# Single-query attention over 256 heads: folding K further on VectorE, and routing the last 16 rows of V past the group sum

## The chip, the cores and the metric

The kernel runs on one core of one Trainium2 chip. The time is that of the device, in microseconds (us), from launch to end of the program on that core; the median over several executions is compared. The times before and after are taken on the same chip. Traces are of one profiled execution.

## What is computed

Attention with one query per head: 8 x 32 = 256 heads, 4096 keys and values of 128 elements, all bfloat16. Each head has its own K and V, so every element is read once (268 MB each) and used in two operations.

```python
def reference(q, k, v):
    scale = q.shape[-1] ** -0.5
    scores = jnp.einsum('bhqd,bhkd->bhqk', q, k) * scale
    attn = _softmax(scores, axis=-1)
    return jnp.einsum('bhqk,bhkd->bhqd', attn, v)
```

## The kernel before

**Tiles.** Eight heads make a tile: the 128 partitions are 8 heads x 16 blocks of keys, and each partition holds C = 256 rows of D = 128 elements, so that one tile of K or V is 8.4 MB. There are NT = 32 tiles t of each kind. Three buffers (`kv_pool`, `SLOTS = 3`) hold K and V tiles in turn: the load order is k0, k1, v0, k2, v1, k3, v2 and so on, and each load reuses the buffer of the load three places before it. So V of tile t goes into the buffer of K of tile t, and K of t+1 into that of V of t-2.

**Scores of a tile.** `product` (L187) multiplies a part of K by the query (L191, VectorE, in place) and folds the products along D: it adds the upper half of the 128 to the lower half (L194), and in the second half of the rows once more (L199), so that 64 or 32 partial products are left per row. `width_of` (L182) says how many. The first and the last three tiles always stop at 64. `sum_over_d` (L206) then adds the remaining partial products on TensorE: it multiplies by the identity and accumulates slices of DS = 8 elements of 64 rows into one PSUM bank (128 x 512, L211), so 8 or 4 matmuls for a quarter of the rows. `scores_of` (L220) reduces the 8 sums that are left per row on VectorE (L223). `weights_of` (L232) takes the maximum (L235 to L242), the exponential on ScalarE (L248) and spreads the weights over eight columns, one per head (L255).

**Values.** `values_loop` (L271, tiles 0 to 28) and `values_of` (L307, the last three) multiply four rows of V at a time by the weights: each matmul has 32 stationary columns and 512 moving ones. In `values_loop` all 64 matmuls are accumulated in one group of 32 columns. In `values_of` successive matmuls go to four column groups, j = 0 to 3, which can run beside one another; in the last tile, the 12 matmuls on rows 128 to 175 all go to group 0 (L315). `copy_of` (L347, ScalarE) brings the sums to SBUF, and `result_of` (L354) adds the groups and picks each head's own part with four small matmuls (L367). `finish_of` (L372) divides by the sum of exponentials on ScalarE, `store_of` (L381) writes to memory from ScalarE's queue.

**The last tile.** V of tile 31 arrives in seven pieces of 128, 64, 32, 16, 8, 4 and 4 rows (`cuts`, L146). Its last LAST = 8 rows don't go through the group sum: GpSimd copies their weights into `w_last` (L261), and eight small matmuls of one row each (L361) add them to the result ahead of the picks (L367).

**Order.** The order within TensorE, VectorE, ScalarE and SP is that of the program text (`manual_schedule`, L392). All loads are issued on SP (L158). In the loop stage (t = 1 to 29) VectorE does `product` on the first half, then on the third quarter, then the reductions of the first two quarters, then `product` on the last quarter and its reductions; TensorE does the sums as they become ready and after the last of them the values loop of the tile before; SP issues K of t+1 when that loop's predecessor has freed its buffer, and V of t when the last sum of K of t is done.

Of the kernel before, what the change touches and what calls it, by code (L numbers as in the profile page):

```python
# [8 lines left out]
ALU = mybir.AluOpType  # L9
AX = mybir.AxisListType  # L10
BF16 = mybir.dt.bfloat16
F32 = mybir.dt.float32
# [3 lines left out]
TG = 4  # L16
R = 2
OB = 4
LAST = 8
LOOP = 6  # L20
EDGE = 2
NEG = -1.0e30
# [3 lines left out]
def kernel(  # L26
# [7 lines left out]
    nc = tc.nc  # L34
    B, H, Sq, D = q.shape
    S = k.shape[2]
    P = nc.NUM_PARTITIONS
# [3 lines left out]
    C = S // PH  # L41
    NT = NH // G
    scale = float(D) ** -0.5
    UC = 64
    DS = 512 // UC
    NU = C // UC
    CB = 4
    RG = R * G
    NQ = NT // R
# [1 line left out]
    AG = CB * G  # L51
    NV = C // CB
    assert (NV - 2 * EDGE) % LOOP == 0
    assert LAST % CB == 0 and TG * AG == P and NH % P == 0 and P % G == 0 and TB % PH == 0 and C % CB == 0

# [12 lines left out]
    ps_s = ctx.enter_context(tc.tile_pool(name="ps_s", bufs=3, space=bass.MemoryType.PSUM))  # L68
# [7 lines left out]
    ident = consts.tile([P, P], BF16, name="ident")  # L76
    nc.gpsimd.memset(ident[:], 0.0)
    nc.gpsimd.affine_select(
        out=ident[:], in_=ident[:], pattern=[[-1, P]], compare_op=ALU.not_equal,
# [6 lines left out]
        out=heads[:], in_=heads[:], pattern=[[-1, G], [0, PH]], compare_op=ALU.not_equal,  # L86
# [6 lines left out]
        out=own[:], in_=own[:], pattern=[[-PH, G]], compare_op=ALU.is_ge,  # L93
# [3 lines left out]
        out=own[:], in_=own[:], pattern=[[PH, G]], compare_op=ALU.is_ge,  # L97
# [14 lines left out]
    for j in range(TG):  # L112
        part = pick[j * AG : (j + 1) * AG, :, :, :]
        nc.gpsimd.affine_select(
            out=part, in_=part, pattern=[[-1, CB], [CB * G, R], [-CB, RG]],
# [6 lines left out]
        out=mine[:], in_=mine[:], pattern=[[PH * G, R], [-PH, RG]], compare_op=ALU.is_ge,  # L122
# [3 lines left out]
        out=mine[:], in_=mine[:], pattern=[[-PH * G, R], [PH, RG]], compare_op=ALU.is_ge,  # L126
        fill=0.0, base=PH - 1, channel_multiplier=-1,
    )

    w_last = consts.tile([P, LAST, RG], BF16, name="w_last")  # L130
    nc.gpsimd.memset(w_last[:], 0.0)
# [4 lines left out]
    def behind_loop(made):  # L136

        if loops:
            tc.add_manual_dep(
                made.ins, loops[-1].name,  # L140
                mybir.DependencyInfo(
                    mybir.DependencyClass.NoSync, mybir.DependencyReason.SCHED_ONLY
                ),
            )
# [2 lines left out]
        ("k", 0): [C // 4, C // 4, C // 2],  # L147
        ("k", NT - 2): [C // 2] * 2,
        ("k", NT - 1): [C // 4, C // 4, C // 2],
        ("v", NT - 1): [C // 2, C // 4, C // 8, C // 16, C // 32, LAST // 2, LAST // 2],  # L150
    }

    def load(kind, t):
# [25 lines left out]
        nc.scalar.activation(out=qb[:, 0, :], in_=qp[:], func=ACT.Copy)  # L179
        qbs[t] = qb  # L180

    def width_of(t, u):  # L182


        return D // 4 if u >= NU // 2 and 0 < t < NT - 3 else D // 2

    def product(t, lo, hi):  # L187
        kt = loads["k", t]
        qb = qbs[t]
        part = kt[:, lo:hi, :]  # L190
        nc.vector.tensor_tensor(  # L191
            out=part, in0=part, in1=qb[:].to_broadcast([P, hi - lo, D]), op=ALU.mult
        )
        nc.vector.tensor_tensor(  # L194
            out=part[:, :, 0 : D // 2], in0=part[:, :, 0 : D // 2],
            in1=part[:, :, D // 2 : D], op=ALU.add,
        )
        if width_of(t, lo // UC) < D // 2:
            nc.vector.tensor_tensor(  # L199
                out=part[:, :, 0 : D // 4], in0=part[:, :, 0 : D // 4],  # L200
                in1=part[:, :, D // 4 : D // 2], op=ALU.add,
            )

    sums = {}

    def sum_over_d(t, u):  # L206
        kt = loads["k", t]
        ps = ps_s.tile([P, UC, DS], F32, name="ps", tag="ps")
        n = width_of(t, u) // DS
        for s in range(n):  # L210
            nc.tensor.matmul(  # L211
                ps[:], lhsT=ident[:],
                rhs=kt[:, u * UC : (u + 1) * UC, s * DS : (s + 1) * DS],
                start=(s == 0), stop=(s == n - 1),
            )
        sums[t, u] = ps

    scs = {}

    def scores_of(t, u):  # L220
        if u == 0:
            scs[t] = sc_pool.tile([P, C], F32, name="sc", tag="sc")
        made = nc.vector.tensor_reduce(  # L223
            out=scs[t][:, u * UC : (u + 1) * UC], in_=sums.pop((t, u))[:], axis=AX.X, op=ALU.add
        )
        if u == NU - 1:
            behind_loop(made)

    ws = {}
# [2 lines left out]
    def weights_of(t):  # L232
# [26 lines left out]
        if t == NT - 1:  # L259
            for i in range(LAST // CB):  # L260
                nc.gpsimd.tensor_copy(  # L261
                    out=w_last[:, i * CB : (i + 1) * CB, RG - G : RG].rearrange("p m g -> p g m"),
                    in_=w[:, (C - LAST) // CB + i, :, :],
                )
# [40 lines left out]
    LT = NT - 3  # L305

    def values_of(t, lo, hi):  # L307
        vt = loads["v", t]
        w = ws[t]
        if lo == 0:  # L310
            avs[t] = ps_v.tile([P, CB * D], F32, name="av", tag="av")
        end = C if t < NT - 1 else C - LAST


        group = [  # L315
            0 if t == NT - 1 and C // 2 <= c0 < C // 2 + 3 * C // 16 else c0 // CB % TG
            for c0 in range(0, end, CB)
        ]
        for c0 in range(lo, hi, CB):
            i = c0 // CB  # L320
            j = group[i]
            nc.tensor.matmul(  # L322
                avs[t][j * AG : (j + 1) * AG, :], lhsT=w[:, i, :, :],
                rhs=vt[:, c0 : c0 + CB, :], start=(i < TG), stop=(j not in group[i + 1 :]),
            )
# [28 lines left out]
    def result_of(t):  # L354
        n, r = divmod(t, R)
        comb = combs.pop(t)
        if r == 0:
            ops[n] = ps_o.tile([RG, D], F32, name="op", tag="op")
        if t == NT - 1:
            for i in range(LAST):  # L360
                nc.tensor.matmul(  # L361
                    ops[n][:], lhsT=w_last[:, i, :], rhs=loads["v", t][:, C - LAST + i, :],
                    start=False, stop=False,
                )
        e = AG if t < LT else P
        for m in range(CB):
            nc.tensor.matmul(  # L367
                ops[n][:], lhsT=pick[0:e, m, r, :], rhs=comb[0:e, m, :],
                start=(r == 0 and m == 0), stop=(r == R - 1 and m == CB - 1),
            )  # L370

    def finish_of(n):  # L372
        s, u = divmod(n, OB)
# [11 lines left out]
            lo = u if (last and u == OB - 1) else 0  # L385
            nc.scalar.dma_start(o_n[s, :, lo : u + 1, :], stages[s][:, lo : u + 1, :])

    Q = C // 4

    load("k", 0)  # L390
    E = mybir.EngineType
    with tc.manual_schedule(engines={E.PE, E.DVE, E.Activation, E.SP}):  # L392
        q_prep(0)
        q_prep(1)
        for t in range(NT):
            loop = 0 < t <= LT
            v_last = t >= NT - 2
            n = t // R - 1
            if not loop:
                if t + 1 < NT:  # L400
                    load("k", t + 1)
                load("v", t)
            product(t, 0, 2 * Q if loop else Q)
            if not loop:
                sum_over_d(t, 0)
            if 0 < t - 1 <= LT:
                if (t - 1) % R == 0:
                    norm_of(n)
                if t > 1:
                    result_of(t - 2)  # L410
            if t + 2 < NT:
                q_prep(t + 2)
            if loop:
                sum_over_d(t, 0)
            else:
                product(t, Q, 2 * Q)
            sum_over_d(t, 1)
            if not loop:
                scores_of(t, 0)
            product(t, 2 * Q, 3 * Q)  # L420
            sum_over_d(t, 2)
            if loop:
                scores_of(t, 0)
            scores_of(t, 1)
            if t > 2 and t % R == 1:
                recip_of(n)
            product(t, 3 * Q, C)
            sum_over_d(t, 3)
            scores_of(t, 2)
            if loop:  # L430
                values_loop(t - 1)
                load("k", t + 1)
                load("v", t)
            if v_last:
                values_of(t - 1, 0, C)
            scores_of(t, 3)
            weights_of(t)
            if t > 2 and t % R == 1:
                finish_of(n)
            if t > 0:  # L440
                copy_of(t - 1)
                if t > 2 and t % R == 1:
                    store_of(n)
                if not loop:
                    if t % R == 0:
                        norm_of(n)
                    result_of(t - 1)
        values_of(NT - 1, 0, C // 2)
        norm_of(NQ - 1)
        recip_of(NQ - 1)  # L450
        values_of(NT - 1, C // 2, C - LAST)
        copy_of(NT - 1)
        result_of(NT - 1)
        finish_of(NQ - 1)
        store_of(NQ - 1)
# [30 lines left out]
```

## Time and profile before

| | us |
|---|---|
| median of 14 runs | 1251.71 (1251.57 to 1252.02) |
| the profiled execution's own time | 1252.92 |
| its span, first to last instruction | 1251.2 |
| VectorE busy | 1021.9 |
| TensorE busy (matmuls; loads of weights 301.1) | 792.6 |
| ScalarE busy | 166.0 |
| bytes read | 536.94 MB, mean 429 GB/s over the span |

The busy times of the engines overlap each other, so they don't add up to the span. A busy share over the whole run says which engine could be the limit; whether it is shows in what it waits for in one period of the loop (some 38.7 us) and in the stretch behind the last load. A DMA load of K or V is shared by 16 DMA engines, each of which adds one to the load's semaphore when its share has landed; the load counts as landed at the sixteenth.

### The profile page before, as it was taken

How to read it: one execution, taken by the hardware profiler on the slowest of the kernel's cores; microseconds unless marked ns; L12 is line 12 of the kernel's file. 1: busy time of each engine (PE TensorE's matmuls, PEld its weight loads, DVE VectorE, ACT ScalarE, POOL GpSimd, SP SyncE). 2: the span in 40 equal slices, each digit the busy share in tenths (PEclk: the TensorE clock that was granted, in tenths of full speed). 3: DMA queues.
4: the chain of work that ended last, by engine and by line, in shares of the span. 5: the costliest groups of instructions: out<-in, count | busy, mean ns of one | idle time of the engine just before them, and what ended most of it. 6: DMA issues, size and time to landing. Idle time of an engine off the chain costs nothing. (4 is left out here: it accounts for less than half of the span.)

```text
span 1251.2 us, 10828 instructions
## 1 busy us (share of the span) xinstructions
PE 792.6 (63%) x3110; PEld 301.1 (24%) x3110; DVE 1021.9 (82%) x495; ACT 166.0 (13%) x433; POOL 4.0 (0%) x22
## 2 busy tenths in 40 slices
PE   2466567655576655766557765577655776656756
PEld 0122122222232222322222222222222222222212
DVE  7887987878977789777798777987779877798783
ACT  0111011111011110111101111011110111101111
POOL 1000000000000000000000000000000000000000
PEclk8687788777887778877788777887877878779866
DMA  9999999999999999999999999999999999999997
GB/s 404 436 436 434 436 434 434 434 436 434 436 422 427 434 436 436 428 434 432 436 436 434 432 436 434 430 430 436 434 434 434 428 433 436 434 434 422 427 438 318
DMA packets 11432, 537.33 MB, mean 429 GB/s; under 512 B 1808, under 2 KB 2064, under 8 KB 2320
## 3 DMA queue, kind: packets, MB, share of 16 engines
q1 hardware_dynamic: 11072, 536.94, 99.4%
q8 instruction: 15, 0.25, 0.1%
q10 hardware_dynamic: 336, 0.07, 0.0%
q14 instruction: 9, 0.07, 0.0%
HBM read 536.94 MB, written 0.07 MB: 429 GB/s over the span
## 5 line engine op out<-in xcount | busy, mean ns | idle before, releaser
L191 DVE TENSOR_TENSOR kt<-kt,qb 128x8192 bf16<-128x8192 bf16 (+1 forms) x99 | 560.9, 5665 | 146.6 <-DMA kt<-in_k_dram 139.9
L211 PE MATMUL ps<-kt,ident 128*128 128x512 bf16 x800 | 282.2, 517 | 385.7 <-DVE kt L199 296.8
L294 PE MATMUL av<-vt,w 128*32 x1740 | 425.2, 396 | 4.6
L194 DVE TENSOR_TENSOR kt<-kt 128x4096 bf16<-128x4096 bf16 (+1 forms) x99 | 288.8, 2917 | 3.4
L294 PEld LDWEIGHTS av<-vt,w 128*32 x1740 | 173.0, 99 | 262.5 <-issue 120.3
L211 PEld LDWEIGHTS <-ident 128*128 128x128 bf16 x800 | 96.8, 121 | 564.4 <-issue 529.4
L223 DVE TENSOR_REDUCE sc<-ps 128x64 f32<-128x512 f32 x128 | 85.3, 685 | 53.5 <-PE ps L211 53.5
L248 ACT ACTIVATE e<-sc,nmax 128x256 bf16<-128x256 f32 x32 | 16.2, 508 | 706.4 <-DVE nmax L242 706.4
L255 ACT ACTIVATE w<-e,mine 128x256 bf16<-128x256 bf16 x256 | 105.6, 495 | 1.1
L199 DVE TENSOR_TENSOR kt<-kt 128x2048 bf16<-128x2048 bf16 x56 | 68.6, 1225 | 1.9
L351 ACT ACTIVATE comb<-av 32x512 bf16<-32x512 f32 (+1 forms) x32 | 18.7, 585 | 330.9 <-PEq L284 321.1
L280 PE MATMUL av<-vt,w 128*32 128x512 bf16 x116 | 47.1, 498 | 14.6 <-issue 13.2
L367 PE MATMUL op<-comb,pick 32*16 32x128 bf16 (+1 forms) x128 | 12.1, 213 | 22.1 <-ACT comb L351 22.1
L280 PEld LDWEIGHTS av<-vt,w 128*32 128x32 bf16 x116 | 6.9, 100 | 54.8 <-issue 54.8
L177 PE MATMUL qp<-qg,heads 8*128 8x128 bf16 x32 | 6.9, 216 | 16.8 <-ACT qg L175 16.8
L322 PE MATMUL av<-vt,w 128*32 128x512 bf16 x190 | 16.4, 423 | 0.8 <-DMA vt<-in_v_dram 0.8
L367 PEld LDWEIGHTS <-pick 32*16 32x16 bf16 (+1 forms) x128 | 8.7, 83 | 29.2 <-issue 28.7
L235 DVE TENSOR_REDUCE pmax<-sc 128x1 f32<-128x256 f32 x32 | 13.4, 420 | 1.1
L175 ACT ACTIVATE qg<-qh 8x128 bf16<-8x128 f32 x32 | 8.5, 266 | 33.5 <-PE qh L171 33.5
L171 PE MATMUL qh<-q_all,ident 128*8 128x128 bf16 x32 | 7.2, 224 | 8.6 <-DMA q_all<-in_q_dram 8.3
L179 ACT ACTIVATE qb<-qp 128x128 bf16<-128x128 f32 x32 | 8.9, 277 | 9.7 <-PE qp L177 9.7
L322 PEld LDWEIGHTS <-w 128*32 128x32 bf16 x190 | 6.9, 103 | 9.8 <-issue 5.9
(31 smaller groups left out, 48.1 us busy)
## 6 DMA issues: line engine op xcount, KB each, us to landing
kt<-in_k_dram SPq DMA_DIRECT2D x4, 4096.0 KB, 24.3
kt<-in_k_dram SPq DMA_DIRECT2D x4, 2048.0 KB, 13.3
vt<-in_v_dram SPq DMA_DIRECT2D x1, 4096.0 KB, 35.0
vt<-in_v_dram SPq DMA_DIRECT2D x1, 2048.0 KB, 39.5
vt<-in_v_dram SPq DMA_DIRECT2D x1, 1024.0 KB, 41.5
vt<-in_v_dram SPq DMA_DIRECT2D x1, 512.0 KB, 42.3
vt<-in_v_dram SPq DMA_DIRECT2D x31, 25.8
kt<-in_k_dram SPq DMA_DIRECT2D x29, 28.3
```

The source lines that it names most:

```text
L191: nc.vector.tensor_tensor(out=part, in0=part, in1=qb[:].to_broadcast([P, hi - lo, D]), op=ALU.mult)
L194: nc.vector.tensor_tensor(out=part[:, :, 0 : D // 2], in0=part[:, :, 0 : D // 2], in1=part[:, :, D // 2 : D], op=ALU.add,)
L199: nc.vector.tensor_tensor(out=part[:, :, 0 : D // 4], in0=part[:, :, 0 : D // 4], in1=part[:, :, D // 4 : D // 2], op=ALU.add,)
L211: nc.tensor.matmul(ps[:], lhsT=ident[:], rhs=kt[:, u * UC : (u + 1) * UC, s * DS : (s + 1) * DS], start=(s == 0), stop=(s == n - 1),)
L223: made = nc.vector.tensor_reduce(out=scs[t][:, u * UC : (u + 1) * UC], in_=sums.pop((t, u))[:], axis=AX.X, op=ALU.add)
L248: nc.scalar.activation(out=e[:], in_=sc[:], func=ACT.Exp, bias=nmax[:, 0:1], scale=scale, accum_out=esums[t // R][:, t % R : t % R + 1],)
L255: nc.scalar.activation(out=w[:, :, g, :], in_=e_g, func=ACT.Copy, scale=mine[:, 0, g : g + 1])
L280: pe.matmul(av, lhsT=wf[:, i * nw : (i + 1) * nw], rhs=vf[:, i * nv : (i + 1) * nv], **how)
L294: pe.matmul(av, lhsT=wf[:, bass.ds(ow + i * nw, nw)], rhs=vf[:, bass.ds(ov + i * nv, nv)], start=False, stop=False,)
L322: nc.tensor.matmul(avs[t][j * AG : (j + 1) * AG, :], lhsT=w[:, i, :, :], rhs=vt[:, c0 : c0 + CB, :], start=(i < TG), stop=(j not in group[ ...
L351: nc.scalar.activation(out=comb[0:n, :, :], in_=av[0:n, :, :], func=ACT.Copy)
L367: nc.tensor.matmul(ops[n][:], lhsT=pick[0:e, m, r, :], rhs=comb[0:e, m, :], start=(r == 0 and m == 0), stop=(r == R - 1 and m == CB - 1),)
```

## The change

It has two parts.

*Folding K.* In tiles 1 to 28 the first half and the last quarter of the rows are folded down to 16 partial products per row, where they were folded to 64 and to 32; the third quarter stays at 32. The sums on TensorE take whole parts: the first half (128 rows) goes into one PSUM bank in slices of BANK / 128 = 4 elements, the quarters in slices of 8 as before. In tiles 1 to 28 the first half then takes 4 matmuls (16 before, for its two quarters), the third quarter 4 (as before), the last 2 (4 before). The scores of the first half are reduced by one instruction where there were two, in tile 29 too.

*The last tile.* LAST is 16: the last 16 rows, in pieces of 8, 4 and 4 rows, go straight into the result. The pieces of the load keep their sizes. The matmuls of the last four rows stand behind the four picks, the other twelve ahead of them. Rows 128 to 151 (6 matmuls) go to column group 0, where it was rows 128 to 175 (12 matmuls); 28 matmuls of the second half go through the group sum, where there were 30.

The diff, without the lines that only rename arguments:

```diff
-LAST = 8
+LAST = 16
...
-    UC = 64
-    DS = 512 // UC
-    NU = C // UC
+    BANK = 512
...
-        ("v", NT - 1): [C // 2, C // 4, C // 8, C // 16, C // 32, LAST // 2, LAST // 2],
+        ("v", NT - 1): [C // 2, C // 4, C // 8, C // 16, LAST // 2, LAST // 4, LAST // 4],
...
-    def width_of(t, u):
-        return D // 4 if u >= NU // 2 and 0 < t < NT - 3 else D // 2
+    def width_of(t, lo):
+        return (D // 4 if lo == C // 2 else D // 8) if 0 < t < NT - 3 else D // 2
...
     def product(t, lo, hi):
...
-        nc.vector.tensor_tensor(
-            out=part[:, :, 0 : D // 2], in0=part[:, :, 0 : D // 2],
-            in1=part[:, :, D // 2 : D], op=ALU.add,
-        )
-        if width_of(t, lo // UC) < D // 2:
+        n = D
+        while n > width_of(t, lo):
+            n //= 2
             nc.vector.tensor_tensor(
-                out=part[:, :, 0 : D // 4], in0=part[:, :, 0 : D // 4],
-                in1=part[:, :, D // 4 : D // 2], op=ALU.add,
+                out=part[:, :, 0:n], in0=part[:, :, 0:n], in1=part[:, :, n : 2 * n], op=ALU.add
             )
...
-    def sum_over_d(t, u):
+    def sum_over_d(t, lo, hi):
         kt = loads["k", t]
-        ps = ps_s.tile([P, UC, DS], F32, name="ps", tag="ps")
-        n = width_of(t, u) // DS
+        ps = ps_s.tile([P, BANK], F32, name="ps", tag="ps")
+        ds = BANK // (hi - lo)
+        n = width_of(t, lo) // ds
         for s in range(n):
             nc.tensor.matmul(
-                ps[:], lhsT=ident[:],
-                rhs=kt[:, u * UC : (u + 1) * UC, s * DS : (s + 1) * DS],
+                ps[:], lhsT=ident[:], rhs=kt[:, lo:hi, s * ds : (s + 1) * ds],
                 start=(s == 0), stop=(s == n - 1),
             )
...
-    def scores_of(t, u):
+    def scores_of(t, lo, hi):
...
+        ps = sums.pop((t, lo))[:].rearrange("p (c s) -> p c s", c=hi - lo)
         made = nc.vector.tensor_reduce(
-            out=scs[t][:, u * UC : (u + 1) * UC], in_=sums.pop((t, u))[:], axis=AX.X, op=ALU.add
+            out=scs[t][:, lo:hi], in_=ps, axis=AX.X, op=ALU.add
         )
...
-            0 if t == NT - 1 and C // 2 <= c0 < C // 2 + 3 * C // 16 else c0 // CB % TG
+            0 if t == NT - 1 and C // 2 <= c0 < C // 2 + 3 * C // 32 else c0 // CB % TG
...
-        if t == NT - 1:
-            for i in range(LAST):
+        def last_rows(lo, hi):
+            for i in range(lo, hi):
                 nc.tensor.matmul(
                     ops[n][:], lhsT=w_last[:, i, :], rhs=loads["v", t][:, C - LAST + i, :],
-                    start=False, stop=False,
+                    start=False, stop=(i == LAST - 1),
                 )
-        e = AG if t < LT else P
+
+        if t == NT - 1:
+            last_rows(0, 3 * LAST // 4)
         for m in range(CB):
             nc.tensor.matmul(
                 ops[n][:], lhsT=pick[0:e, m, r, :], rhs=comb[0:e, m, :],
-                start=(r == 0 and m == 0), stop=(r == R - 1 and m == CB - 1),
-            )
+                start=(r == 0 and m == 0), stop=(r == R - 1 and m == CB - 1 and t < NT - 1),
+            )
+        if t == NT - 1:
+            last_rows(3 * LAST // 4, LAST)
...
-            product(t, 0, 2 * Q if loop else Q)
-            if not loop:
-                sum_over_d(t, 0)
+            if loop:
+                product(t, 0, HALF)
+            else:
+                product(t, 0, Q)
+                sum_over_d(t, 0, Q)
...
-                sum_over_d(t, 0)
+                sum_over_d(t, 0, HALF)
...
-            sum_over_d(t, 1)
...
             if loop:
-                scores_of(t, 0)
-            scores_of(t, 1)
+                scores_of(t, 0, HALF)
+            else:
+                scores_of(t, Q, HALF)
```

More of the change, by code (lines that the diff above doesn't have):

```diff
@@ L193, in product @@
         )
-        nc.vector.tensor_tensor(
-            out=part[:, :, 0 : D // 2], in0=part[:, :, 0 : D // 2],
-            in1=part[:, :, D // 2 : D], op=ALU.add,
-        )
-        if width_of(t, lo // UC) < D // 2:
+        n = D
+        while n > width_of(t, lo):
+            n //= 2
             nc.vector.tensor_tensor(
-                out=part[:, :, 0 : D // 4], in0=part[:, :, 0 : D // 4],
-                in1=part[:, :, D // 4 : D // 2], op=ALU.add,
+                out=part[:, :, 0:n], in0=part[:, :, 0:n], in1=part[:, :, n : 2 * n], op=ALU.add
             )
     sums = {}
-    def sum_over_d(t, u):
+    def sum_over_d(t, lo, hi):
         kt = loads["k", t]
-        ps = ps_s.tile([P, UC, DS], F32, name="ps", tag="ps")
-        n = width_of(t, u) // DS
+        ps = ps_s.tile([P, BANK], F32, name="ps", tag="ps")
+        ds = BANK // (hi - lo)
+        n = width_of(t, lo) // ds
         for s in range(n):
             nc.tensor.matmul(
-                ps[:], lhsT=ident[:],
-                rhs=kt[:, u * UC : (u + 1) * UC, s * DS : (s + 1) * DS],
+                ps[:], lhsT=ident[:], rhs=kt[:, lo:hi, s * ds : (s + 1) * ds],
                 start=(s == 0), stop=(s == n - 1),
             )
-        sums[t, u] = ps
+        sums[t, lo] = ps
     scs = {}
-    def scores_of(t, u):
-        if u == 0:
+    def scores_of(t, lo, hi):
+        if lo == 0:
             scs[t] = sc_pool.tile([P, C], F32, name="sc", tag="sc")
+        ps = sums.pop((t, lo))[:].rearrange("p (c s) -> p c s", c=hi - lo)
         made = nc.vector.tensor_reduce(
-            out=scs[t][:, u * UC : (u + 1) * UC], in_=sums.pop((t, u))[:], axis=AX.X, op=ALU.add
+            out=scs[t][:, lo:hi], in_=ps, axis=AX.X, op=ALU.add
         )
-        if u == NU - 1:
+        if hi == C:
             behind_loop(made)
@@ L358, in result_of @@
             ops[n] = ps_o.tile([RG, D], F32, name="op", tag="op")
-        if t == NT - 1:
-            for i in range(LAST):
+        e = AG if t < LT else P
+        def last_rows(lo, hi):
+            for i in range(lo, hi):
                 nc.tensor.matmul(
                     ops[n][:], lhsT=w_last[:, i, :], rhs=loads["v", t][:, C - LAST + i, :],
-                    start=False, stop=False,
+                    start=False, stop=(i == LAST - 1),
                 )
-        e = AG if t < LT else P
+        if t == NT - 1:
+            last_rows(0, 3 * LAST // 4)
         for m in range(CB):
@@ L386, in store_of @@
             nc.scalar.dma_start(o_n[s, :, lo : u + 1, :], stages[s][:, lo : u + 1, :])
-    Q = C // 4
+    Q, HALF = C // 4, C // 2
     load("k", 0)
@@ L413 @@
             if loop:
-                sum_over_d(t, 0)
+                sum_over_d(t, 0, HALF)
             else:
-                product(t, Q, 2 * Q)
-            sum_over_d(t, 1)
-            if not loop:
-                scores_of(t, 0)
-            product(t, 2 * Q, 3 * Q)
-            sum_over_d(t, 2)
+                product(t, Q, HALF)
+                sum_over_d(t, Q, HALF)
+                scores_of(t, 0, Q)
+            product(t, HALF, HALF + Q)
+            sum_over_d(t, HALF, HALF + Q)
             if loop:
-                scores_of(t, 0)
-            scores_of(t, 1)
+                scores_of(t, 0, HALF)
+            else:
+                scores_of(t, Q, HALF)
             if t > 2 and t % R == 1:
                 recip_of(n)
-            product(t, 3 * Q, C)
-            sum_over_d(t, 3)
-            scores_of(t, 2)
+            product(t, HALF + Q, C)
+            sum_over_d(t, HALF + Q, C)
+            scores_of(t, HALF, HALF + Q)
             if loop:
@@ L435 @@
                 values_of(t - 1, 0, C)
-            scores_of(t, 3)
+            scores_of(t, HALF + Q, C)
             weights_of(t)
```

## The prediction

> **What bounds the kernel now.** I read the busy shares and slices, the DMA queues, the waits of VectorE, one period of the timeline, the groups by shape, and the timeline of the end. Slices first:
>
> ```profile
> PE 792.6 (63%) x3110; PEld 301.1 (24%) x3110; DVE 1021.9 (82%) x495; ACT 166.0 (13%) x433; POOL 4.0 (0%) x22
> ...
> DMA  9999999999999999999999999999999999999997
> GB/s 404 436 436 434 436 434 434 434 436 434 436 422 427 434 436 436 428 434 432 436 436 434 432 436 434 430 430 436 434 434 434 428 433 436 434 434 422 427 438 318
> ```
>
> No engine is full, but the DMA is, from the first slice to the last but one. The queues say what fills it:
>
> ```profile
> q1 hardware_dynamic: 11072, 536.94, 99.4%
> q8 instruction: 15, 0.25, 0.1%
> q14 instruction: 9, 0.07, 0.0%
> ```
>
> q1 carries K and V. The other two fetch instructions and matter below. Does the DMA ever wait for a buffer? One period of the loop:
>
> ```profile
> 624.77 8.69 DVE L191 TENSOR_TENSOR kt<-kt,qb 128x16384 bf16<-128x16384 bf16 x1 [4.87 <-DMA kt<-in_k_dram]
> ...
> 653.73 1.23 DVE L199 TENSOR_TENSOR kt<-kt 128x2048 bf16<-128x2048 bf16 x1
> ...
> 655.01 1.86 PE L211 MATMUL ps<-kt,ident 128*128 128x512 bf16 x4 [8.10 <-DVE kt L199]
> ...
> 656.91 0.33 SPq L158 DMA_DIRECT2D vt<-in_v_dram  x1
> ...
> 663.48 8.69 DVE L191 TENSOR_TENSOR kt<-kt,qb 128x16384 bf16<-128x16384 bf16 x1 [4.90 <-DMA kt<-in_k_dram]
> ```
>
> VectorE waits 4.9 us for K in each period of 38.7 us. V's load is issued at 656.91, when the last sum has freed the slot; the K ahead of it in the queue lands at 663.36 (its semaphore), so the queue has 6.45 us of work left. At the start of the run the first packet moved 1.0 us after its issue (0.81 to 1.82). So the stream never runs dry, and the time is the stream, its start, and what follows the last bytes:
>
> ```profile
> 1241.47 5.88 PE L322 MATMUL av<-vt,w 128*32 128x512 bf16 x30 [0.84 <-DMA vt<-in_v_dram]
> 1247.19 0.61 PE L361 MATMUL op<-vt,w_last 128*16 128x128 bf16 x8
> 1247.46 0.60 ACT L351 ACTIVATE comb<-av 128x512 bf16<-128x512 f32 x1 [9.86 <-PE av L322]
> 1248.11 0.38 PE L367 MATMUL op<-comb,pick 128*16 128x128 bf16 x4 [0.31 <-ACT comb L351]
> 1248.53 0.36 ACT L376 ACTIVATE stage<-op,rz 16x128 bf16<-16x128 f32 x1 [0.47 <-PE op L367]
> ```
>
> The semaphores of the last V tile's pieces of 64, 32, 16, 8, 4 and 4 rows fill at 1241.42, 1243.90, 1245.14, 1245.79, 1246.15 and 1246.45. TensorE starts on the 64 rows at once and is late from then on: it gets to the 32 rows at 1246.33. The end hangs on the landing of the 64 rows and on TensorE's steps.
>
> **What the Trainium skill says.** (1) "VectorE: DVE Perf Modes", What auto-detection actually checks: two 16-bit operands of step 1 run at two results per cycle. The groups by shape agree:
>
> ```profile
> L194 DVE TENSOR_TENSOR kt<-kt 128x4096 bf16<-128x4096 bf16 x70 | 160.5, 2292 | 2.4
> L194 DVE TENSOR_TENSOR kt<-kt 128x8192 bf16<-128x8192 bf16 x29 | 128.3, 4425 | 1.0
> L223 DVE TENSOR_REDUCE sc<-ps 128x64 f32<-128x512 f32 x128 | 85.3, 685 | 53.5 <-PE ps L211 53.5
> L199 DVE TENSOR_TENSOR kt<-kt 128x2048 bf16<-128x2048 bf16 x56 | 68.6, 1225 | 1.9
> ```
>
> 0.52 ns an element and 0.16 us fixed, with rows of 64 and of 32 elements alike. (2) "SBUF — State Buffer", Door 1: The DMA port swizzle, its note on 16-byte lines: at least two hits in a line keep full rate. The new first-half sum reads runs of four bf16, 8 bytes; no row of before shows that, all read 16 bytes. (3) "TensorE: Matmul & The Clock Gate", Part 1: half clock until about 3.4 us of sustained work. Here the array goes from 0.427 to 0.216 us a step of 512 columns at 1245.65, 4.2 us after 1241.47. (4) "Runtime: NRT & Kernel Launch", Instruction fetch mechanics: 64-byte instructions, fetched ahead by DMA, cost mostly hidden. Here the engine hides it, the DMA doesn't, as the next part shows.
>
> **The change, part by part.** *VectorE in the loop (28 periods).* Two more adds on the first half (4096 and 2048 elements: 2.29 + 1.22), one on the last quarter (1024: 0.16 + 0.53 = 0.69), one reduction of 512 PSUM elements fewer (0.60 start to start): +3.6 us. Cover: the 4.9 us of waiting, of which 1.3 stay. Bounds: 0 saved on the reduction if outputs count, and double price for rows of 16 elements; I take the fitted line, since 64 and 32 lie on it.
>
> *TensorE in the loop.* 24 sums become 10 (4 + 4 + 2). The 14 saved lie beside VectorE, except two at the end of the last quarter: 0.85 us earlier. Bounds of the 8-byte runs: full or half rate; even half (1.7 us for four) hides behind the next 4.42 us product. Tile 29 keeps 16 of them; at half rate it would delay V by up to 3.4 us, where 7.7 are spare (issue 1160.9, K lands 1168.6). I take full rate.
>
> *Queued behind it.* V's issue on SP moves by 3.51 - 0.60 + 0.69 - 0.85 = +2.75 us, its lead falls from 6.45 to 3.7, still over 1.0. The values loop and the next K issue behind it on TensorE and SP move by the same; K is issued at 635.04 for a landing at 643.99, lead 9.0 to 6.2. Price: nothing.
>
> *Instructions.* This one shows in the packets and in each load's sixteen semaphore increments, one per DMA engine. q14's 8 KB packets come at 145.7, 417.6, 706.4 and 997.7, when VectorE has run 63, 185, 317 and 448 instructions by the trace: 8 KB is 128 instructions of 64 bytes. Each throws one and the same DMA engine back by 0.97 us: its lag behind the first engine is 0.2 at 80.9, 1.16 at 159.7, 2.15 at 450, 3.13 at 742 and 4.11 at 1033. That engine ends every load from 417 on, so each fetch is 0.97 us on the path. (TensorE's 15 fetches rotate over others, about 1.45 us each, and stay below it; fewer of them gain nothing.) The compiled lists hold 527 VectorE instructions before and 582 after; the trace's 563 become about 618. The next fetch would be near 577: not reached before, reached after, some 40 instructions from the end, around 1155 us. Cost: +0.97 us on every landing of the last tile. Bounds: 0 (the fetch isn't made, or lands on another engine) and 0.97.
>
> *The end.* The pieces keep their sizes. Before, 12 matmuls share a column group and 18 follow four at a time: 17 steps, ten gaps cold (0.38 + 9 x 0.427) and six warm (0.216), 1241.47 to 1246.97. After: 6 alone, 22 in fours, 11 steps, so six fewer. From 1241.47 the last would start at 1245.69, and with the sums behind at before's distances (ACT's copy +0.48, the picks +0.65) the picks at 1246.82. The four new matmuls behind them cost 4 x 0.056 = 0.22. The result copy starts at 1247.47 for 1248.53: -1.06. With all landings 0.97 later: start 1242.44, last step 1246.2 (rows landed 1246.11, clock warm from 1245.65), copy 1246.7 to 1247.3, but the first eight direct rows land at 1246.76 and the next four at 1247.12, so these matmuls run to 1247.47, the picks to 1247.70, the last four (landed 1247.42) start up to 1247.87, the result copy at 1248.13: -0.40 us. GpSimd makes two more copies of 0.23 us at 1237, nine us early; its larger memset at 2.1 us is covered too.
>
> **Sum.** -1.06 at the end, +0.66 of it given back by the fetch: -0.40. The span goes 1251.2 to 1250.8; the profiled run 1252.92 lies 1.21 over the median 1251.71, so the median goes to 1251.3.
>
> **Rivals.** (a) No fifth fetch on the late engine: -1.06, 1250.6. For: nothing in before shows it; against: four even fetches and the count. (b) TensorE stays cold at the end, since its work starts 0.2 us into the clock's window: steps 0.427 to the last, at 1246.66, the eight small matmuls 0.107 each, result copy near 1249.15: +0.6, 1252.3. Against: a window with 0.2 idle of 3.4 still looks busy. (c) The other side: VectorE becomes the bound in the loop. If rows of 16 cost double, the adds come to 2.29 + 2.28 + 1.22 - 0.60 = 5.2 us, over the 4.9 it has. V's lead (6.45 - 4.3 - 1.0 = 1.1) lasts four periods, then 24 x 0.3 = 7 us: 1259. It decides from 4.9 us on; against it stand the two shapes on one line. (d) The change doesn't do what it says because the landing of the last rows binds: no gain, 1251.7; against: 1246.45 stands two us ahead of the result copy.
>
> **Chances.** Forecast 1251.3: 0.50, alone 1250.9 to 1251.8. (a) 0.27, (b) 0.10, (c) 0.08, (d) 0.05. The range 1250.2 to 1252.8 takes in all but (c) and some scatter. About 0.2% (2.5 us) is what a measurement of this kernel tells from no change: faster 0.03, same 0.88, slower 0.09, mostly (c).
>
> **What would show it.** Right: VectorE waits about 1.3 us per K, V issued about 3.7 us before K lands, a fifth 8 KB fetch near 1155 us, the 64 rows landing near 1242.4, eleven steps on them and the rest, DMA slices as before. Wrong: a 1024-element add over 0.8 us, landings near 1241.4, VectorE's wait for K gone, slices below 430 GB/s in the loop.

## The result, and the profile after

| | before | after |
|---|---|---|
| median, us | 1251.76 (1251.54 to 1252.91, 28 runs) | 1266.77 (1264.51 to 1268.79, 6 runs) |
| ratio, 95% interval | | 1.012 [1.011, 1.013] |
| profiled execution, its span | 1252.92, 1251.2 | 1268.11, 1266.4 |
| VectorE busy, TensorE busy | 1021.9, 792.6 | 1122.4, 689.3 |

The kernel is 15.0 us slower, far outside the forecast of 1251.3 (1250.2 to 1252.8). The page of the changed kernel, its busy times, slices and queues:

```profile
PE 689.3 (54%) x2724; PEld 250.0 (20%) x2724; DVE 1122.4 (89%) x550; ACT 166.2 (13%) x433; POOL 4.5 (0%) x24
...
GB/s 400 443 435 435 433 429 410 428 425 433 435 427 420 429 416 443 412 433 426 423 429 412 428 422 420 428 426 429 429 426 431 429 404 431 431 431 411 433 441 345
...
q1 hardware_dynamic: 11072, 536.94, 99.1%
q8 instruction: 12, 0.20, 0.1%
...
q14 instruction: 10, 0.08, 0.0%
```

Same bytes, same 11072 packets, but the slices dip to 404 to 412 GB/s in the loop, where before the lowest there was 422. q1 was in packets for 99.4% of 1251.2 = 1243.7 us before, and for 99.1% of 1266.4 = 1255.0 now. So of the 15.2 us of span about 11.3 are packets that took longer, and 3.9 are engines without a packet. (The shares are rounded, so each figure is good to about 1 us.) The loss is in the stream, all along the loop.

VectorE isn't the limit. Its groups by shape, and its wait for K (us in total, times, longest):

```profile
L195 DVE TENSOR_TENSOR kt<-kt 128x4096 bf16<-128x4096 bf16 x98 | 224.7, 2292 | 3.3
...
L195 DVE TENSOR_TENSOR kt<-kt 128x2048 bf16<-128x2048 bf16 x84 | 102.9, 1225 | 2.9
...
L219 DVE TENSOR_REDUCE sc<-ps 128x128 f32<-128x512 f32 x29 | 19.8, 684 | 0.0
L195 DVE TENSOR_TENSOR kt<-kt 128x1024 bf16<-128x1024 bf16 x28 | 19.4, 691 | 1.0
```

```profile
DVE kt L189 <- DMA kt<-in_k_dram: 74.4, 28, 4.6
```

The adds take what was forecast, and the one reduction of the first half takes as long as each of the two did before (0.68 us). VectorE still waits 74.4 / 28 = 2.7 us for each K, more than the 1.3 forecast: K comes some 0.5 us later in each period, and VectorE waits less for TensorE's sums (30.8 us in all, 53.5 before, so 0.8 a tile), which the forecast left out of this wait. One period, by its timeline:

```profile
587.43 0.69 DVE L195 TENSOR_TENSOR kt<-kt 128x1024 bf16<-128x1024 bf16 x1
...
588.18 1.03 PE L207 MATMUL ps<-kt,ident 128*128 128x512 bf16 x2 [7.35 <-DVE kt L195]
589.25 0.33 SPq L156 DMA_DIRECT2D vt<-in_v_dram  x1
...
592.88 8.69 DVE L189 TENSOR_TENSOR kt<-kt,qb 128x16384 bf16<-128x16384 bf16 x1 [1.96 <-DMA kt<-in_k_dram]
```

V is issued at 589.25 and K ahead of it lands at 592.81: lead 3.56, as forecast (3.7). Yet this V's last sixteenth lands 22.09 us after K's, not 19.35 as in a full stream, and the K behind it comes 2.7 us late. The next periods show it at VectorE:

```profile
592.88 8.69 DVE L189 TENSOR_TENSOR kt<-kt,qb 128x16384 bf16<-128x16384 bf16 x1 [1.96 <-DMA kt<-in_k_dram]
634.25 8.69 DVE L189 TENSOR_TENSOR kt<-kt,qb 128x16384 bf16<-128x16384 bf16 x1 [4.61 <-DMA kt<-in_k_dram]
672.92 8.69 DVE L189 TENSOR_TENSOR kt<-kt,qb 128x16384 bf16<-128x16384 bf16 x1 [1.97 <-DMA kt<-in_k_dram]
```

41.37 us for one period and 38.67 for the next. What happened at 589.25 is in the packets. The first of the sixteen DMA engines had finished K 1.06 us after V's issue (its increment of K's semaphore), the last 3.56 after. V's first packets start at 590.23. Of the first twelve, seven take 2.97 to 3.51 us and three 2.58 to 2.84, where a packet of 64 KB in the stream takes 2.42. Over the run 461 of these packets take more than 2.5 us (29 before), 376 of them within 6 us of an issue of V; what they take over 2.42, divided by sixteen engines, is 12.9 us (0.9 before). So V is issued ahead of the *last* engine's end of K, but too late for the engines that are ahead, and when several start again together their packets are slow. (The next K is issued later too, with 7.4 us to the last engine of V in the mean, 9.1 before. But it has at worst 6.1 us to the last and 4.3 to the first, and K's first and last increments come 19.37 and 19.35 us behind V's: nothing is lost there.)

The end of the changed kernel, by the timeline:

```profile
1258.06 4.22 PE L318 MATMUL av<-vt,w 128*32 128x512 bf16 x28 [2.87 <-DMA vt<-in_v_dram]
...
1262.40 0.60 ACT L347 ACTIVATE comb<-av 128x512 bf16<-128x512 f32 x1 [9.46 <-PE av L318]
1262.40 0.83 PE L359 MATMUL op<-vt,w_last 128*16 128x128 bf16 x12
...
1263.07 0.39 PE L367 MATMUL op<-comb,pick 128*16 128x128 bf16 x4
...
1263.29 0.39 PE L359 MATMUL op<-vt,w_last 128*16 128x128 bf16 x4
1263.72 0.36 ACT L378 ACTIVATE stage<-op,rz 16x128 bf16<-16x128 f32 x1 [0.72 <-PE op L359]
```

From the landing of the 64 rows (1258.02) to the result copy it is 5.70 us, before 7.11; the end is 3.38 us behind the last landing, before 4.77.

### The profile page after: what moved, and what is told of

It reads as the page before. It is cut to its first block, busy times and chain, and to the rows that moved or that the text cites. A ratio compares the mean times of both kernels' runs of the same rounds, so it can differ in the third digit from the quotient of the medians.

```text
span 1266.4 us, 10145 instructions
## 1 busy us (share of the span) xinstructions
PE 689.3 (54%) x2724; PEld 250.0 (20%) x2724; DVE 1122.4 (89%) x550; ACT 166.2 (13%) x433; POOL 4.5 (0%) x24
## 3 DMA queue, kind: packets, MB, share of 16 engines
q1 hardware_dynamic: 11072, 536.94, 99.1%
## 5 line engine op out<-in xcount | busy, mean ns | idle before, releaser
L189 DVE TENSOR_TENSOR kt<-kt,qb 128x8192 bf16<-128x8192 bf16 (+1 forms) x99 | 560.8, 5665 | 81.1 <-DMA kt<-in_k_dram 74.4
L195 DVE TENSOR_TENSOR kt<-kt 128x8192 bf16<-128x8192 bf16 (+2 forms) x239 | 475.3, 1989 | 8.1
L207 PE MATMUL ps<-kt,ident 128*128 128x512 bf16 x408 | 177.9, 586 | 505.1 <-DVE kt L195 504.8
L290 PEld LDWEIGHTS av<-vt,w 128*32 x1740 | 176.8, 102 | 259.9 <-issue 108.2
L207 PEld LDWEIGHTS <-ident 128*128 128x128 bf16 x408 | 41.9, 123 | 634.2 <-DVE kt L195 568.3
L219 DVE TENSOR_REDUCE sc<-ps 128x64 f32<-128x512 f32 (+1 forms) x99 | 67.9, 686 | 30.8 <-PE ps L207 30.8
L367 PE MATMUL op<-comb,pick 32*16 32x128 bf16 (+1 forms) x128 | 12.1, 213 | 21.3 <-ACT comb L347 21.3
L233 DVE TENSOR_SCALAR spread<-same,pmax 128x32 f32<-128x32 f32 x32 | 7.7, 241 | 1.1
```

The costliest lines, as they stand in the source:

```text
L189: nc.vector.tensor_tensor(out=part, in0=part, in1=qb[:].to_broadcast([P, hi - lo, D]), op=ALU.mult)
L195: nc.vector.tensor_tensor(out=part[:, :, 0:n], in0=part[:, :, 0:n], in1=part[:, :, n : 2 * n], op=ALU.add)
L207: nc.tensor.matmul(ps[:], lhsT=ident[:], rhs=kt[:, lo:hi, s * ds : (s + 1) * ds], start=(s == 0), stop=(s == n - 1),)
L219: made = nc.vector.tensor_reduce(out=scs[t][:, lo:hi], in_=ps, axis=AX.X, op=ALU.add)
L290: pe.matmul(av, lhsT=wf[:, bass.ds(ow + i * nw, nw)], rhs=vf[:, bass.ds(ov + i * nv, nv)], start=False, stop=False,)
L367: nc.tensor.matmul(ops[n][:], lhsT=pick[0:e, m, r, :], rhs=comb[0:e, m, :], start=(r == 0 and m == 0), stop=(r == R - 1 and m == CB - 1 an ...
```

## The experiments

The theory from these readings is *late issue*: V's issue must lie far enough ahead of the DMA engine that finishes K first, and the change moved it past that point. Rivals: *VectorE's time* (each us that it works longer counts), *traffic* (the narrow adds, or sums over 8-byte runs, disturb the transfers), and *fetches* of instructions. A further rival is TensorE's clock: the share of it that was granted fell from 0.80 before to 0.72. Ratios are against the kernel before, on the same chip; the experiments ran on several chips, whose medians of before are 1251.76 to 1251.92, so that the chip itself adds some 0.2 us to a comparison of medians.

**1. The last tile's edits alone** (`LAST`, the pieces, column group 0, four rows behind the picks; nothing folded).

> Only the last tile's part of the change (16 direct rows, six matmuls in one column group, the last four rows behind the picks); K is folded as before. My prediction's sum for the end without a further instruction fetch: 1.06 us less, 1250.7. If the last landing binds (about 0.3 us from it to the last matmul, in place of the two us of before): 1.4 us less, 1250.4. If the end is the cause of the loss: 1266.

Measured: 1251.71, before 1251.92, ratio 0.9998 [0.9989, 1.0007]. No gain that can be told. The timeline of its end:

```profile
1241.19 1.89 PE L322 MATMUL av<-vt,w 128*32 128x512 bf16 x16 [1.09 <-DMA vt<-in_v_dram]
1243.72 0.61 PE L322 MATMUL av<-vt,w 128*32 128x512 bf16 x8 [0.65 <-DMA vt<-in_v_dram]
1244.96 0.40 PE L322 MATMUL av<-vt,w 128*32 128x512 bf16 x4 [0.62 <-DMA vt<-in_v_dram]
1245.61 0.83 PE L363 MATMUL op<-vt,w_last 128*16 128x128 bf16 x12 [0.25 <-DMA vt<-in_v_dram]
```

Here TensorE ran warm from the start (at the higher of its two clocks, 0.216 us a step of 512 columns; cold is 0.427) and waits for each piece; the landings bind. The profiled execution of before was cold there, and 1.2 us above its median; 26 of its 28 runs lie at 1252.03 or below. How the old tail looks when most of it is warm is in the profile of experiment 7:

```profile
1246.85 0.39 PE L323 MATMUL av<-vt,w 128*32 128x512 bf16 x2 [0.24 <-DMA vt<-in_v_dram]
1247.19 0.70 PE L362 MATMUL op<-vt,w_last 128*16 128x128 bf16 x8
```

TensorE waits for the rows there too, and the span ends 3.8 us behind the last landing, as in experiment 1. That the runs of before near its median were warm in the same way is inferred from this; no profile of such a run was taken.

**2. The folding alone** (the changed kernel with the last tile as before).

> Only the deeper folding of K; the end as before. If the folding causes the whole loss and the end is worth 1.1 to 1.4 us: 1267.9 to 1268.2. If the two parts interact: clearly below 1267 or above 1269.

Measured: 1267.65 (1264.76 to 1269.42, 4 runs), ratio 1.0123 [1.0106, 1.0140]. The folding is the whole loss.

**3. The changed kernel, V in two halves.** V goes into the place of its own K, so its first half can be issued when the sums of K's first half are done.

```diff
-    kv_pool = ctx.enter_context(tc.tile_pool(name="kv_pool", bufs=SLOTS))
+    kv_pool = ctx.enter_context(tc.tile_pool(name="kv_pool", bufs=1))
...
-        buf = kv_pool.tile([P, C, D], BF16, name=f"{kind}t", tag="kv")
+        own = kind == "v" and 0 < t < NT - 2
+        if own:
+            buf = loads["k", t]
+        else:
+            place = max(2 * t - 1, 0) if kind == "k" else 2 * t + 2 - (t == NT - 1)
+            buf = kv_pool.tile([P, C, D], BF16, name=f"{kind}t", tag=f"kv{place % SLOTS}")
...
-        for n in cuts.get((kind, t), [C]):
+        for n in cuts.get((kind, t), [C // 2] * 2 if own else [C]):
```

> The changed kernel, with V of tiles 1 to 29 loaded into the buffer of its K in two halves, the first issued when the first half's sums are done, some 20 us before the K ahead lands. All work on VectorE and TensorE stays, only the issue is earlier. Late issue (the queues of the engines that are ahead run dry): the loss is gone, 1250.5 to 1251.5, no packet of 64 KB or 32 KB stretched at the turn from K to V. Traffic (VectorE's further adds, or TensorE's reads of 8 bytes, slow the transfers): the loss stays, 1265 to 1268.

Measured: 1254.86 (1254.68 to 1255.1, 10 runs), ratio 1.0024 [1.0014, 1.0034]. 12 of the 15 us come back with all of the folding kept, so neither VectorE's time nor the traffic is the cause. Nor is TensorE's clock: its granted share was 0.73 here, and 0.79 in experiment 4, which has the loss. The rest: V in halves takes 2 x 9.71 = 19.42 us for 19.35, times 29 is 2.0, and a fifth fetch of VectorE's instructions moves the last landing by 0.97.

**4. The kernel before, V later by a useless instruction.** One partition, 2480 elements, 2.71 us, ahead of the last quarter.

```diff
+            if 0 < t < NT - 3:
+                nc.vector.tensor_reduce(
+                    out=idle[:], in_=mine[0:1, 0, 0:1].to_broadcast([1, 2480]), axis=AX.X, op=ALU.add
+                )
             product(t, 3 * Q, C)
```

> The kernel before, with one reduction on a single partition (2480 elements read from one address, about 2.75 us) ahead of the last quarter's product in tiles 1 to 28: V is issued as late as in the changed kernel, with no traffic to speak of and no change on TensorE. Late issue: the loss of the changed kernel less what the end gains, 1264 to 1270. Traffic: 1251.7 to 1252.7, since 28 more instructions stay below a fifth fetch (577), or just reach it.

Measured: 1265.57 (1263.52 to 1268.51, 4 runs), ratio 1.0105 [1.0088, 1.0122]. The loss is there without any folding, but VectorE works nearly as long as in the changed kernel (1095.5 us, 1122.4 there).

**5. The same instruction, behind the issue.** It stands after `weights_of(t)`, in the time in which VectorE waits for the next K.

> The kernel before, with the same useless reduction of 2480 elements (2.7 us) in tiles 1 to 28, but placed after the weights of the tile, where VectorE waits for the next K and V's load is already issued. VectorE does the same work as in the run that gave 1265.57, so its wait for K falls from 6.3 us in the mean by the same 2.7. Late-issue theory: nothing is lost, 1251.7 to 1252.2 us (with a fetch if 28 more instructions reach one: none, since there are as many as in the run with the pad ahead). If it is VectorE's load, or its short wait for K, that costs: 1264 to 1266 us.

Measured: 1253.46 (1252.53 to 1253.76, 20 runs), ratio 1.0011 [1.0005, 1.0018]. The busy times and the slices of experiment 4, then of experiment 5:

```profile
PE 759.2 (60%) x3110; PEld 291.9 (23%) x3110; DVE 1095.5 (86%) x523; ACT 166.0 (13%) x433; POOL 4.0 (0%) x22
...
GB/s 399 445 441 433 424 429 425 420 430 433 432 425 428 431 428 433 431 425 408 422 429 429 410 435 425 430 429 433 426 427 435 430 421 410 428 431 408 431 441 316
```

```profile
PE 781.9 (62%) x3110; PEld 299.9 (24%) x3110; DVE 1094.7 (87%) x523; ACT 166.0 (13%) x433; POOL 4.0 (0%) x22
...
GB/s 404 436 436 434 436 434 434 436 433 434 436 434 423 432 430 436 436 434 431 429 433 434 436 436 430 436 434 434 427 434 436 433 434 434 427 432 422 429 442 309
```

The same 523 instructions and the same busy time, in another place: 12.1 us. This is the cleanest pair. The expectation missed one thing: 28 more instructions do reach a fifth fetch (after those at 145.8 and 417.7 they come at 667.8, 939.7 and 1216.7 us, where before had two more, 706.4 and 997.7). It moves the last landing to 1247.49, 1.04 later than before; the other 0.5 of the 1.55 us stands against an end of 4.4 us behind the landing, with TensorE cold.

**6. The kernel before, V in two halves** (the edit of experiment 3).

> The kernel before, with V of tiles 1 to 29 loaded in two halves into its own K's place, and nothing folded. This is the price of the split alone. Late-issue theory (the change lost its 15 us because V was issued too late; the split gives it back and costs 29 x 0.07 us for the smaller packets): 1253.7 to 1254.0 us, no fifth 8 KB fetch of VectorE, and the kernel changed and split (1254.86) lies above it by about that fetch, 1 us. If the split's gain comes from something else, such as a generally better order of loads, this kernel is faster than before: under 1251.2.

Measured: 1255.77 (1255.18 to 1255.93, 7 runs), ratio 1.0029 [1.0018, 1.0041]. Higher than expected: here too VectorE records 28 instructions more than before (591 for 563) and makes a fifth fetch. The last landing is 1249.41, 2.96 later than before: 2.0 for the halves and 0.97 for the fetch. The end is 4.6 us behind it. So the split is no gain in itself; it only mends the late issue.

**7 and 8. A smaller pad ahead of the last quarter** (800 elements, 0.96 us; 1760 elements, 1.96 us).

> The kernel before, with one useless reduction of one partition and 800 elements (about 1.0 us) on VectorE ahead of the last quarter's product in tiles 1 to 28. V is issued 1.0 us later. Late-issue theory: before, V is issued at worst 2.3 us ahead of the first of the 16 DMA engines that runs out of K, and this loses nothing; with 1.3 at worst and about 2.5 in the mean only the later tiles, where the engines stand furthest apart, lose: 1252 to 1255 us. A theory of VectorE's time (every us it works longer counts): 28 x 1.0 x (13.8 / 75.9), that is 5 us: 1257.

> As the run with 1.0 us, with 1760 elements (about 2.0 us). Late-issue theory: a loss that grows faster than the pad, since more tiles fall under the lead at which an engine runs dry: 1256 to 1261 us, against 1265.6 for 2.7 us of pad. A theory of VectorE's time, in proportion: 1261.5 to 1262.

Measured: 1253.36 (1252.68 to 1253.72, 20 runs), ratio 1.0010 [1.0003, 1.0017], and 1258.32 (1254.8 to 1259.78, 4 runs), ratio 1.0055 [1.0038, 1.0072]. Both have the fifth fetch, so they compare with experiment 5: nothing for the first us (the last landing is at 1247.47, 1247.49 there), 4.9 for two, 12.1 for 2.7. The four runs with two us scatter over 5.0 us. A price in proportion to VectorE's time is out.

**9. Folding the first half once only** (to 32 elements a row).

```diff
-        return (D // 4 if lo == C // 2 else D // 8) if 0 < t < NT - 3 else D // 2
+        return D // 4 if 0 < t < NT - 3 else D // 2
```

> The kernel changed, with the first half of K added down to 32 elements a row only (one more add of 4096 elements than before, not two) and the last quarter to 32 as before. V is issued 2.29 - 0.60 = 1.7 us later than before, and VectorE has as many instructions as before, so four 8 KB fetches. Late-issue theory: with 1.0 us of pad nothing was lost beside a fifth fetch and its effect at the end (1253.36 against 1253.46 for the pad behind), with 2.0 us 4.9, with 2.7 us 12.1; so 1.7 us costs 1 to 4: 1252.5 to 1256 us. A theory in which the folding itself (its reads, writes or the sums over 8-byte runs) costs in proportion to the adds: 2.29 of 4.2 us more adds, so 8 of the 15 us: 1259 to 1260.

Measured: 1253.91 (1251.99 to 1257.47, 20 runs), ratio 1.0018 [1.0011, 1.0025]. More than half of the extra adding costs 2 us of the 15.

**10. Folding the last quarter only.** The first half stays at 64, in one bank, with sums over 8-byte runs.

```diff
-        return (D // 4 if lo == C // 2 else D // 8) if 0 < t < NT - 3 else D // 2
+        return (D // 2 if lo == 0 else D // 4 if lo == C // 2 else D // 8) if 0 < t < NT - 3 else D // 2
```

> The kernel changed, with the first half of K added down to 64 elements a row as before, and only the last quarter to 16. The first half's sum still fills one bank with 16 matmuls over 8-byte runs, and is reduced at once. V is issued 0.60 - 0.69 + 0.85 = 0.76 us earlier than before; 28 adds come in and 28 reductions go, so four fetches. Late-issue theory: nothing lost, and the end of the changed kernel: 1251.4 to 1251.9 us. A theory in which the narrow adds or the 8-byte runs disturb K's and V's transfers: over 1254.

Measured: 1251.55 (1251.32 to 1251.78, 12 runs), before 1251.76, ratio 0.9997 [0.9988, 1.0005]. The narrow adds and the 8-byte runs cost nothing when V is issued early. It is the fastest kernel of the study, but not told apart from before.

**11. A pad of 3560 elements** (3.83 us), to see the slope.

> The kernel before, with a useless reduction of 3560 elements (about 3.8 us) ahead of the last quarter's product in tiles 1 to 28. Late-issue theory: the first engine has run out of K in every tile when V is issued, so from here on each further us of delay costs nearly a us in each of 28 tiles: 12.1 + 2.5 us at 2.7 of pad, about 1.1 x 28 = 31 more: 1285 to 1300 us. If the loss were one of spreading or of a fixed price for each late issue, it would level off: 1268 to 1275.

Measured: 1278.51 (1274.38 to 1279.75, 4 runs), ratio 1.0204 [1.0182, 1.0225]. 13 us more than with 2.7, neither 31 nor levelled off. Both branches of my expectation were wrong, and the traces say why. V is issued a fixed time after the landing of its own K (32.27 us before, 36.02 here), so a loss in one tile makes the period longer and gives the next issue that much more lead. From issues and semaphore increments of each profiled execution, means over tiles 1 to 28 in us. The delay is that of V's issue behind its own K, less 32.27. The loss a tile is the span less 1251.9, the span of experiment 5, or less 1249.9, that of experiment 10, for 9, which has no fifth fetch; divided by 28. (Experiment 8's profile is of its fastest run, 1254.8; its median makes the loss 0.17.)

| | delay | lead over K's last engine | over the first | loss a tile | lead + loss |
|---|---|---|---|---|---|
| experiment 10 | -0.71 | 7.26 | 4.70 | 0 | |
| before | 0 | 6.57 | 4.09 | 0 | |
| 7 (0.96 us) | 0.88 | 5.68 | 3.25 | 0 | |
| 9 (first half once) | 1.75 | 4.90 | 2.69 | 0.12 | 5.0 |
| 8 (1.96 us) | 1.88 | 4.78 | 2.82 | 0.04 | 4.8 |
| 4 (2.71 us) | 2.63 | 4.44 | 1.97 | 0.53 | 5.0 |
| after | 2.90 | 4.22 | 1.84 | 0.52 | 4.7 |
| 11 (3.83 us) | 3.75 | 3.75 | 1.34 | 0.88 | 4.6 |

Wherever there is a loss, lead and loss add up to 4.6 to 5.0 us. With a delay d of the issue the lead is 6.57 - d + loss; so the loss a tile is about half of what 6.57 - d lacks of that sum. With 4.8 for the sum and the delay of experiment 11 this gives 0.99 x 28 = 28 us, somewhat more than the 25 measured. It is a rule fitted to these runs.

Which lead counts can be read from the same traces. Take the 28 tiles of each of the twelve profiles in which V is loaded whole (336 tiles), and call the loss of a tile the time from the mean of K's sixteen increments to the mean of V's, over 19.35. By the lead over the first engine it is:

| lead over the first engine, us | under 1 | 1 to 2 | 2 to 2.5 | 2.5 to 3 | 3 and more |
|---|---|---|---|---|---|
| tiles | 19 | 57 | 60 | 58 | 142 |
| mean loss, us | 1.32 | 0.74 | 0.37 | 0.14 | 0.05 |

With the lead over the last engine held between 4 and 5 us, the loss still goes from 0.62 (1 to 2 us to the first) to 0.08 (3 and more). For 2 to 2.5 us to the first it is 0.48 where the last engine has under 4.5 us and 0.20 where it has over 5.5, so the others count too, but less.

**12. The changed kernel with one instruction moved.** A test of the rule, made before the run.

```diff
             product(t, HALF, HALF + Q)
             sum_over_d(t, HALF, HALF + Q)
-            if loop:
-                scores_of(t, 0, HALF)
-            else:
+            if not loop:
                 scores_of(t, Q, HALF)
...
             sum_over_d(t, HALF + Q, C)
+            if loop:
+                scores_of(t, 0, HALF)
             scores_of(t, HALF, HALF + Q)
```

> The kernel changed, with one instruction moved: the reduction of the first half's scores (0.68 us) stands behind the product of the last quarter instead of ahead of it, in tiles 1 to 28. Nothing is added or taken away, VectorE does the same work in each tile, and V is issued about 0.65 us earlier. From the runs so far: lead of V's issue over K's last landing plus loss per tile is about 5.0 us wherever there is a loss, and a delay of the issue by d gives a lead of 6.7 - d + loss; so the loss per tile is half of what 6.7 - d lacks of 5.0. For the change d is 2.86 and the loss 0.58 x 28 = 16; with d = 2.2 it is 0.25 x 28 = 7. Late-issue theory with this rule: 9 us less than the kernel changed, 1257.7, within 1255 to 1260 us. A theory of VectorE's work, of the folding's traffic or of the fetches: 1265 to 1268 as before the move.

Measured: 1258.3 (1254.97 to 1262.12, 6 runs), ratio 1.0054 [1.0036, 1.0073]. 8.5 us come back from moving 0.68 us of work behind the issue, none of it removed; in the profile V is issued 0.61 us earlier than in the changed kernel (34.56 us behind its own K, 35.17 there). The rule said 9. It had the difference right and both losses too large: 16 and 7 us, where the medians lie 13.3 and 4.8 above that of experiment 5. (Its 6.7 and 5.0 came from means that were not all taken over tiles 1 to 28; the table has them.)

## Why the prediction was wrong

**The step that failed** is in the part on what is queued behind VectorE: "its lead falls from 6.45 to 3.7, still over 1.0. [...] Price: nothing." The first half was right (4.2 in the mean, 0.5 of which the loss itself gives back; 3.56 in the period shown). The 1.0 was wrong, twice over. It was the time from issue to first packet with all engines idle at the start of the run, and it still is that (589.25 to 590.23). (The Trainium skill, "DMA: Bandwidth & Descriptors", Latency and other measured facts, gives about 0.6 us to the first byte for loads issued like this; with that number the step fails in the same way.) But the lead was counted to the semaphore's sixteenth increment, the *last* engine, while the prediction itself had found the engines up to 4.1 us apart. The first engine finishes 1.8 us behind the issue in the mean, and at worst before it. And the stream loses although the first engine has more than the 0.98 us to the first packet: of the changed kernel's tiles 1 to 28, the first increment of V comes 0.17 us late in the 7 with over 2.3 us to the first engine, 0.45 in the 12 with 1.5 to 2.3 us, and 1.28 in the 9 with less. Before, the worst of these tiles had 2.32 (4.09 in the mean). The kernel stood at that edge at its worst tiles, and the profile showed it: the increments were read for the fetches, not for the lead.

**VectorE's costs** were right: 2.29, 1.22 and 0.69 us a kind of add, one reduction fewer, full rate on rows of 16. **TensorE's sums** over 8-byte runs took 1.89 us for four, as those over 16 bytes, but that is with TensorE cold. In experiment 10 many of them run warm, at 0.216 us a step, so the 8-byte runs have full rate there too. **Delay of the issue**: 2.75 forecast, 2.90 measured.

**The fifth fetch** came: q14's packets of VectorE lie at 125.7, 384.1, 661.8, 913.3 and 1168.0 us, the last forecast near 1155. Its price of 0.97 us on the landings is what experiments 3, 5 and 6 show. In the changed kernel itself it can't be told beside the loss.

**The end** was mis-sized. -1.06 us was worked out from an execution in which TensorE was cold, 1.2 us above the median; experiment 1 measures -0.2, inside its interval. Rival (d), that the landing of the last rows binds, is what experiments 1 and 7 show where TensorE is warm. In the changed kernel the end was shorter (3.38 us behind the last landing), but TensorE's state differs between executions, and experiment 2 less the change (0.9 us, within a scatter of 4) doesn't settle it.

**The rivals.** (c) had the sign and the place, V's lead in the loop, and 1259 us, with a chance of 0.08. Its mechanism is not what happened: no add cost double, and VectorE kept waiting for K. A rival that priced the lead against the first engine was missing. The sign to look for was named, slices below 430 GB/s in the loop, and it is what the page shows, though less sharply than it was put: before itself had six such slices in the loop, the lowest 422.

**Still open**: why packets are slow for one or two rounds when several engines start again together. That they are is shown; experiment 4 shows that no folding is needed for it, and experiment 5 that VectorE's load alone doesn't bring it. Why a lead of up to 3 us to the first engine is needed, when a first packet comes 0.98 us after its issue, is open with it. A version with equal engines and a late issue wasn't tried.

## What to carry to other kernels

Where a DMA stream is the bound, the issue of the next load has a due time, and work ahead of it on any engine is on the path although that engine waits later: place work behind the issue, as experiments 5 and 12 did. Count the lead to the DMA engine that finishes first, in the worst tile, and take as safe only what the kernel is seen to bear (here 3.25 us to the first engine in the mean and 2.15 at worst, in experiment 7). An idle 4.9 us of VectorE said nothing on that.

## What the runs showed of the hardware

- Each 8 KB fetch of VectorE's instructions costs one DMA engine 0.97 us in a full stream, and always the same engine by the lag that grows in the increments, so before's four leave it 4.1 us behind the first; a fifth moved the last landing by 1.04 us (experiment 5). 28 more VectorE instructions, even in idle time, were enough for it.
- A restart isn't only a gap. About three quarters of the loss (11.3 of 15.2 us) were packets that took longer than 2.42 us (up to 3.51 in the restart shown), the rest engines without a packet.
- A load that is late in every period costs about half of what its lead lacks, by the rule above, because the period that it stretches gives lead back: 1.1 us more delay a tile (experiment 11 against 4) cost 13 us, not 31.
- A load of 8.4 MB in two halves takes 19.42 us for 19.35.
